# First FFT of a fused FFT-filter and squared-ReLU feed-forward kernel: later filter loads, crossed filter pieces by DMA, six zero matmuls, stage A of batch 1 in bank pairs

## The chip, the cores and the metric

The kernel runs on one core of a Trainium2 chip. Time is the device time of one launch in microseconds (us); the figure to be moved is the median over several launches. The core has five engines that run side by side, each through its own list of instructions in order: TensorE (PE, matmuls into PSUM), VectorE (DVE), ScalarE (ACT), GpSimd (POOL) and SyncE (SP). DMAs are issued from the lists of SP, ACT and POOL and carried by 16 DMA engines. A DMA issued by POOL can convert float32 to float16 on the way; one issued by SP can't. An instruction that waits for a semaphore holds back everything behind it in its engine's list.

## What is computed

The input `x` has 8 batches of 3008 tokens with 256 channels. Each batch is transformed along its tokens, multiplied by a complex filter, transformed back, and the result goes token by token through a feed-forward layer with a squared ReLU:

```python
def _attn_ref(x, filt_r, filt_i):
    X = np.fft.rfft(x, axis=1)
    F = (filt_r + 1j * filt_i)[None, :, :]
    Y = X * F
    y = np.fft.irfft(Y, n=x.shape[1], axis=1)
    return y.astype(np.float32)

def _moe_ref(x, w_in, w_out):
    h = np.maximum(x @ w_in, 0.0)
    return (h * h @ w_out).astype(np.float32)

# x (8, 3008, 256), filt_r and filt_i (1505, 256), w_in (256, 2048), w_out (2048, 256)
# out = _moe_ref(_attn_ref(x, filt_r, filt_i).reshape(24064, 256), w_in, w_out)
```

## The kernel before

**The transform.** 3008 = 64 x 47, so the transform is done in two steps, all by matmuls in float16. Stage A sums over the 47 (result `u`), stage B over the 64 (result in PSUM tile `psB`, with real and imaginary parts on the two halves of the partitions). `unit_b(b, p)` (L378) does stage B for two of the 24 frequency classes, p = 0 to 11, and multiplies by the filter tile `sF` into `prod`. `sF` is `[128, 2, 24, 256]`: in `sF[:, 0]` the real part lies on partitions 0 to 63 and the imaginary part on 64 to 127; in `sF[:, 1]` the two halves are crossed. Stage P (`unit_p0` for batch 0, `unit_p` for the others) goes back from frequencies, gives `ze`, and writes it to DRAM (`dZ`); `read_z` (L450) reads it back in another order into two tiles `zt`, and `unit_y` (L458) does the last step into `yt`, which holds a batch's transformed tokens.

**The feed-forward layer.** Tokens go in 47 groups of 512. Eight steps per group: `ffn_g1` (L486) makes 256 of the 2048 hidden channels in `psH`, ACT applies the ReLU (L506), DVE squares every second step (`ffn_sq`, L513); the output product of a group runs in the eight steps of the next group. Group 0's is `ffn_g2` (L515): step 8 uses the first half of `sWout`, step 9 the second half. Later groups use a seven-product scheme (`make_t`, `sums`, `products`). Group 0 needs units 0 to 3 of `unit_y`, the first step of group 1 needs units 4 to 7.

**The order of the work.** There is no scheduler: the order in which the code runs is the order of each engine's list. What is ahead of the loop at L741 is the prologue: batch 0's transform, three quarters of batch 1's stage A, and the first four `unit_y`. `fft_plan` (L641) puts all the other transform work at half steps of the loop: a unit with number r runs in step floor(r), in its first or second place. `fixed` units have their place; `moves` (loads, stores, small DVE work) ride along.

In detail, where the change touches it:

- **Loads at the start.** SP issues batch 0's input in six pieces of 512 KB (`load_wide`, L207; pieces go to the wide tiles `xw32[0]`, `[1]`, `[2]`, in the order of `HALVES`, L278), then the constants `sC1`, `sSB`, `sSP`, `sSPx` (L281 to L286). POOL's list begins with a one-element copy `tiny` (L288) that waits for the fourth of these pieces, the second half of `xw32[1]`, and holds POOL's list back until then. After it POOL issues the filter (`load_f`, L235: 18 DMAs, four class ranges `FC` = 0-6, 6-12, 12-18, 18-24), then batch 1's `x` (`load_x`) and the first half of `sWin`.
- **`turn_f`** (L245): two DVE copies of 64 partitions x 1536 elements fill `sF[:, 1]` for a range of classes from `sF[:, 0]`; called for a range just ahead of the first unit that uses it (p = 0, 3, 6, 9; L717 to L719).
- **`unit_b` for batch 0:** `psB` is copied to `ub` by ACT (L395), then DVE multiplies `ub` by both planes of `sF` (L397). `psB` takes its bank from `psF` where p % 4 is 0 or 1 and from `psO` where it is 2 or 3, two buffers each. `turn_u(k)` (L355) turns stage A's result for two p at a time and sits between the units on PE; `turn_u(2)` takes the two `psF` banks that units 0 and 1 had.
- **`settle_f`** (L251): once batch 0 has used `sF`, two DVE instructions per three classes rewrite it to the form the other batches use. All eight are `moves` in steps 1 to 8.
- **Stage A of batch 1:** `unit_a` (L316) does one of 16 slices: one matmul of 512 columns into one `psF` bank, one copy out, by ACT and DVE in turn; after each fourth slice the chunk `u` is written to DRAM (`write_u`). Slices 0 to 11 run in the prologue, 12 to 15 in steps 8 and 9. `bank_pair` (L163) hands out pairs of banks, in turn from `psH`, `psH`, `psF`, `psO`; `pair_engine` names ACT and DVE alternately.
- **`load_rest`** (L294) is behind `read_z` on POOL: a one-element copy waits for the first half of the first `zt`, then POOL issues the second half of `sWin`, the rest of batch 1's `x`, and the two halves of `sWout`.
- **`fill(n)`** (L303): n matmuls on a tile of zeros, whose result nothing reads.

Of the kernel before, what the change touches and what calls it, by code (L numbers as in the profile page):

```python
# [9 lines left out]
F16 = mybir.dt.float16  # L10
# [94 lines left out]
def kernel(  # L105
# [9 lines left out]
    nc = tc.nc  # L115
    B, S, D = x.shape
# [128 lines left out]
    def turn_f(c0, c1):  # L245

        for i in (0, 64):
            nc.vector.tensor_copy(out=sF[i:i + 64, 1, c0:c1, :],
                                  in_=sF[64 - i:128 - i, 0, c0:c1, :])

    def settle_f(c0, c1):  # L251

# [32 lines left out]
        load_const(sSP[:, c, :], dPA, k)  # L285
        load_const(sSPx[k], dPB, k)  # L286
    tiny = const.tile([1, 2], F16, name="tiny")
    nc.gpsimd.tensor_copy(out=tiny[:, 0:1], in_=xw32[1][0:1, 4, 0:1])  # L288
    for c in FC:
        load_f(*c)  # L290
    for k in range(2):
# [24 lines left out]
    def unit_a(b, a):  # L316

        c, i = divmod(a, 4)
        if i == 0:
            us[(b, c)] = p_u.tile([96, 8, D], F16, tag="u", name=f"u_{b}_{c}")  # L320
        ps = psF(f"psA_{b}_{a}")
        m = slice(2 * i, 2 * i + 2)
        nc.tensor.matmul(ps[0:96, :], sSA, x16s[(b, c)][0:94, m, :], start=True, stop=True)  # L323
        o = us[(b, c)][:, 2 * i:2 * i + 2, :]
        pv = ps[0:96, :].rearrange("p (a d) -> p a d", d=D)
        if a % 2 == 0 or b > 2:
            nc.scalar.copy(out=o, in_=pv)  # L327
        else:
            nc.vector.tensor_copy(out=o, in_=pv)
        if i == 3:  # L330
            write_u(b, c)

    def chunk_a0(k, *cs):

# [43 lines left out]
    def unit_b(b, p):  # L378
        if b == 0 and p % 4 > 1:
            ps = psO(f"psB_{b}_{p}").rearrange("p a d -> p (a d)")  # L380
        else:
            ps = psF(f"psB_{b}_{p}")
        for i in range(2):
            nc.tensor.matmul(ps[:, i * D:(i + 1) * D], sSB[:, 2 * p + i, :],  # L384
                             uts[b][:, 2 * p + i, :], start=True, stop=True)
        if b == 0:
            if p == 0:
                prods["ring"] = p_y.tile([128, 5, 2, 2, D], F16, tag="yt", name="prods_0")
            prod = prods["ring"][:, p % 5]
        else:  # L390
            prod = p_prod.tile([128, 2, 2, D], F16, tag="prod", name=f"prod_{b}_{p}")
        pv = ps.rearrange("p (a d) -> p a d", d=D)
        if b == 0:
            ub = p_prod.tile([128, 2, D], F16, tag="prod", name=f"ub_{p}")
            nc.scalar.copy(out=ub, in_=pv)  # L395
            pv = ub
        nc.vector.tensor_mul(  # L397
            out=prod,
            in0=pv.unsqueeze(1).to_broadcast([128, 2, 2, D]),
            in1=sF[:, :, 2 * p:2 * p + 2, :])  # L400
        prods[(b, p)] = prod
        if b > 0:
            for i in range(2):
                nc.gpsimd.dma_start(out=prod[64 * i:64 * i + 64, 0],  # L404
                                    in_=prod[64 - 64 * i:128 - 64 * i, 1],
                                    accum_op=mybir.AluOpType.add)
# [234 lines left out]
    def fft_plan():  # L641

        fixed, units, moves = [], [], []
        for b in range(1, B):
            f = (b * S // TG) * SLOTS - (48 if b > 1 else 40)
            d = 0
            if b == 1:
                for n in range(4, 16):
                    fixed.append(((n if n < 8 else n + 2 if n < 12 else 2 * n - 7) + n % 2 / 2,
                                  unit_y, 0, n))  # L650
                moves.append((7.5, read_z, 0, 3))
                for q in range(8):
                    moves.append((1 + q, settle_f, 3 * q, 3 * q + 3))
                moves.append((10, settle_sp))
                for a in range(12, 16):
                    fixed.append((2 + a / 2, unit_a, b, a))
                moves.append((10.5, read_u, b))
                d = 7
            else:
                for a in range(16):  # L660
                    if a % 2 == 0 and b > 2:
                        moves.append((f + ((-57 + 2.3 * a) if b == 3 else (-66 + 2.75 * a)),
                                      load_x, b, a // 2))
                    units.append((f + (-16 + a, -46 + 2.1 * a, -56 + 2.75 * a)[min(b, 4) - 2],
                                  unit_a, b, a))
                moves.append((f + (2 if b == 2 else -6.5), read_u, b))
            for p in range(12):
                r = 14 + 15 * p / 11 if b == 1 else 6 + 28 * p / 11 if b == 2 else -2 + 36 * p / 11
                units.append((f + r, unit_b, b, p))
                if b == 1 and 2 <= p < 10:  # L670
                    moves.append((f + r, load_x, 2, p - 2))
                units.append((f + r + (4.5 if b == 1 else 7 - 2.5 * p / 11), unit_p, b, p))
            for c in range(4):
                moves.append((f + (40 + d / 14, 43, 48, 54)[c] - d, read_z, b, c))
            for n in range(16):
                (fixed if n < 4 else units).append((f + YN[n] - d, unit_y, b, n))
        work, used, done = {}, set(), {}
        for r, *u in fixed:
            h = int(2 * r)
            used.add(h)  # L680
            work.setdefault(h, []).append(u)
        rank = (unit_b, unit_p, unit_y, unit_a)
        for r, *u in sorted(units, key=lambda u: (rank.index(u[1]), u[0])):
            after = done.get((u[0], u[1]), -1)
            h = min((h for h in range(max(int(2 * r) - 3, after + 1), int(2 * r) + 12)
                     if h not in used),
                    key=lambda h: (sum(h + i in used for i in (-2, -1, 1, 2)) > 2) * 2
                    + abs(h - int(2 * r)))
            used.add(h)
            done[(u[0], u[1])] = h  # L690
            work.setdefault(h, []).append(u)
        for r, *u in moves:
            work.setdefault(int(2 * r), []).append(u)
        return work
# [7 lines left out]
    for n, cs in enumerate(((0, 2), (0, 2), (1, 3), (1, 3))):  # L702
# [1 line left out]
            cast_wide(*h)  # L704
        chunk_a0(n % 2, *cs)
        if n < 2:
            fill(4 - 2 * n)
    uts[0] = p_ut.tile([128, NC, D], F16, tag="ut", name="ut_0")
    for k in range(2, 6):
        load_x(1, k)  # L710
    load_win(0)
    turn_u(0, nc.scalar, nc.vector)
    turn_u(1, nc.scalar, nc.vector)
    for k in range(8):
        if k < 6:
            for p in (2 * k, 2 * k + 1):
                for c in FC:  # L717
                    if c[0] == 2 * p:
                        turn_f(*c)  # L719
                if k > 1 and p % 2:  # L720
                    unit_p0(k - 2)
                unit_b(0, p)
# [4 lines left out]
    read_z(0, 0)  # L727
    read_z(0, 1)
    load_rest()
    for a in range(12):  # L730
        unit_a(1, a)
    fill(6)
    for n in range(4):
        unit_y(0, n)
    prologue[0] = False
# [53 lines left out]
```

## Time and profile before

| | us |
|---|---|
| median of 7 runs | 770.32 |
| lowest, highest | 769.25, 772.43 |
| the profiled execution, its own time | 771.0 |
| its span from first to last instruction | 769.2 |
| first feed-forward matmul (start of L502) | 52.18 |
| first matmul of group 0's output product (L522) | 65.98 |

| engine | busy us | share of the span |
|---|---|---|
| PE | 742.9 | 97% |
| DVE | 647.1 | 84% |
| ACT | 572.0 | 74% |
| POOL | 187.8 | 24% |

The mean granted clock of PE is 0.991 of full speed. The times above are counted from the start of the span, in the one profiled execution. All that the change edits lies in the first 78 us or so; from there on the span is the loop over groups. Between the span and the execution's own time lie 1.8 us.

### The profile page before, as it was taken

The page shows a single profiled execution, that of the slowest core. Times are in us where ns is not written, and L with a number is a line of the kernel's source. Part 1 is how long each engine was busy: PE and PEld are TensorE (multiplying, and loading weights), DVE is VectorE, ACT ScalarE, POOL GpSimd, SP SyncE. Part 2 cuts the span into 40 slices and gives each one's busy share as a digit, 9 for nine tenths or more (in the row PEclk, how much of TensorE's full clock was granted, in tenths as well). Part 3 has the DMA queues.
Part 4 walks back from the last instruction along what each step waited for, and adds up shares of the span by engine and source line. Part 5 has one row for each costly group of instructions (what it writes and reads, how often), then busy time and mean ns, then how long its engine had stood idle before and what let it go on. Part 6 is the DMA issues. An engine that isn't in the chain of part 4 may idle for free.

```text
span 769.2 us, 19455 instructions
## 1 busy us (share of the span) xinstructions
PE 742.9 (97%) x8138; PEld 544.3 (71%) x8138; DVE 647.1 (84%) x735; ACT 572.0 (74%) x842; POOL 187.8 (24%) x262
## 2 busy tenths in 40 slices
PE   6778999999999999999999999999999999999998
PEld 4535667777777777877778777787777777777776
DVE  4847998899889888898979889788989989888783
ACT  2756777788878887788877877778877777777773
POOL 3420561133303232223212324043311222000000
PEclk9989999999999999999999999999999999999999
DMA  9996798667676456855586565865447334321011
GB/s 314 174 213 142 163 182 211 203 115 142 134 203 143 100 120 148 214 118 94 125 214 136 104 135 103 200 144 118 101 105 209 91 77 97 96 71 55 29 57 56
DMA packets 107184, 104.87 MB, mean 136 GB/s; under 512 B 9960, under 2 KB 94504, under 8 KB 106200
## 3 DMA queue, kind: packets, MB, share of 16 engines
q1 hardware_dynamic: 82408, 77.80, 34.0%
q0 software_dynamic: 24544, 25.64, 24.4%
q8 instruction: 64, 1.05, 0.6%
q10 hardware_dynamic: 144, 0.18, 0.1%
q14 instruction: 24, 0.20, 0.1%
HBM read 58.95 MB, written 48.23 MB: 139 GB/s over the span
## 4 chain that ended last, share of the span: by engine, by line
PE 82%; DVE 9%; DMA 5%; ACT 2%; issue 1%; SPq 0%; POOL 0%; ACTq 0%; DVEq 0%
PE psH L502 36%; PE psX L615 18%; PE psY L615 14%; PE psA L323 3%; DMA zt<-dZ 3%; PE psY L472 2%; PE psB L384 2%; DVE h L513 2%; PE psP L436 2%; DVE prod L397 2%; PE psO L522 2%; PE fill L307 1%; DMA prod<-prod 1%; DVE sum L588 1%; ACT h L506 1%
## 5 line engine op out<-in xcount | busy, mean ns | idle before, releaser
L506 ACT ACTIVATE h<-psH 128x1024 f16<-128x1024 f32 x376 | 384.5, 1024 | 153.9 <-PE psH L502 151.8
L502 PE MATMUL psH<-yt,sWin 128*128 128x512 f16 (+7 forms) x1728 | 387.5, 352 | 3.6 <-DVE yt L481 2.9
L513 DVE TENSOR_TENSOR h<-h 128x2048 f16<-128x2048 f16 (+1 forms) x192 | 229.8, 1197 | 45.9 <-ACT h L506 45.6
L404 POOL DMA_DIRECT2D prod<-prod x168 | 139.4, 972 | 433.3 <-DVE prod L397 393.1
L502 PEld LDWEIGHTS <-sWin 128*128 128x128 f16 x1728 | 152.2, 98 | 100.3 <-issue 6.2
L615 PEld LDWEIGHTS <-sum 128*128 128x128 f16 x2880 | 177.6, 98 | 20.2 <-issue 0.3
L615 PEld LDWEIGHTS <-h 128*128 128x128 f16 x2160 | 133.7, 98 | 21.3
L397 DVE TENSOR_TENSOR prod<-psB,sF 128x1024 f16<-128x1024 f32 x84 | 102.4, 1219 | 14.5 <-PE psB L384 14.3
L615 PE MATMUL psX<-sT,sum 128*128 128x128 f16 x1440 | 102.4, 219 | 0.0
L615 PE MATMUL psY<-sT,sum 128*128 128x128 f16 x720 | 69.6, 219 | 0.0
L327 ACT CAST u<-psA 96x512 f16<-96x512 f32 x96 | 55.7, 580 | 6.2 <-PE psA L323 5.8
L591 DVE TENSOR_TENSOR sum<-sum,h 128x2048 f16<-128x2048 f16 x45 | 55.0, 1222 | 1.0
L615 PE MATMUL psY<-sWout,h 128*128 128x128 f16 x720 | 55.0, 219 | 0.0
L615 PE MATMUL psY<-sWout,sum 128*128 128x128 f16 x720 | 54.7, 219 | 0.2 <-DVE bot L630 0.2
L615 PE MATMUL psX<-sT,h 128*128 128x128 f16 x720 | 54.9, 219 | 0.0
L597 DVE TENSOR_TENSOR sum<-h,sum 128x2048 f16<-128x2048 f16 x45 | 54.8, 1217 | 0.0
L594 DVE TENSOR_TENSOR sum<-h 128x2048 f16<-128x2048 f16 x45 | 54.8, 1217 | 0.0
L588 DVE TENSOR_TENSOR sum<-h 128x2048 f16<-128x2048 f16 x45 | 54.7, 1216 | 0.0
L481 DVE CAST yt<-psY 128x376 f16<-128x376 f32 x62 | 33.7, 544 | 21.6 <-PE psY L472 21.6
L438 ACT CAST ze<-psP 128x512 f16<-128x512 f32 x84 | 49.1, 585 | 1.0 <-PE psP L436 0.7
L615 PE MATMUL psX<-sWout,h 128*128 128x128 f16 x720 | 47.6, 219 | 0.0
L472 PEld LDWEIGHTS <-zt 112*128 112x128 f16 x512 | 34.2, 99 | 18.3 <-issue 3.4
(70 smaller groups left out, 600.9 us busy)
## 6 DMA issues: line engine op xcount, KB each, us to landing
zt<-dZ SPq DMA_DIRECT2D x64, 192.0 KB
dU<-u SPq DMA_DIRECT2D x28, 384.0 KB
prod<-prod POOLq DMA_DIRECT2D x168, 64.0 KB, 2.8
dZ<-ze SPq DMA_DIRECT2D x28, 384.0 KB
x<-in_x_dram POOLq DMA_DIRECT2D x48, 192.0 KB, 5.0
ut<-dU SPq DMA_DIRECT2D x7, 1024.0 KB
out_dram<-top SPq DMA_DIRECT2D x31, 128.0 KB
out_dram<-bot SPq DMA_DIRECT2D x31, 128.0 KB
```

The lines of the kernel that those rows point to most:

```text
L327: nc.scalar.copy(out=o, in_=pv)
L397: nc.vector.tensor_mul(out=prod, in0=pv.unsqueeze(1).to_broadcast([128, 2, 2, D]), in1=sF[:, :, 2 * p:2 * p + 2, :])
L404: nc.gpsimd.dma_start(out=prod[64 * i:64 * i + 64, 0], in_=prod[64 - 64 * i:128 - 64 * i, 1], accum_op=mybir.AluOpType.add)
L472: nc.tensor.matmul(ps[:, 94 * jj:94 * jj + 94], zt[:, 4 * (g % 2) + jj, dt * 128:(dt + 1) * 128], sSY, start=True, stop=True)
L502: nc.tensor.matmul(ps[:, i, o:o + n], sWin[:, dt, jt * 128:(jt + 1) * 128], yts[b][:, dt, r:r + n], start=(dt == 0), stop=(dt == 1))
L506: nc.scalar.activation(out=h2[:, 2 * s:2 * s + 2, :], in_=ps, func=AF.Relu)
L513: nc.vector.tensor_mul(out=v, in0=v, in1=v)
L588: nc.vector.tensor_add(out=t, in0=a21, in1=a22)
L591: nc.vector.tensor_sub(out=t, in0=f[5], in1=a11)
L594: nc.vector.tensor_sub(out=t, in0=a11, in1=a21)
L597: nc.vector.tensor_sub(out=t, in0=a12, in1=f[6])
L615: nc.tensor.matmul(o[:, t, :], f[p][:, q, 128 * t:128 * t + 128], sg["w"][p][:, q, :], start=(m == 0 and p in (1, 2)), stop=(q == 7), skip ...
```

## The change

The edits, in the order of the program:

- `tiny` now waits for the sixth and last piece of batch 0's `x` instead of the fourth.
- `turn_f` for all four ranges is called once, ahead of the units of stage B. The first range is still copied by DVE; the other three become two DMAs each, issued from SP's list (six DMAs of 192 KB, SBUF to SBUF).
- `unit_b` for batch 0 runs one matmul on zeros (512 columns) into its bank ahead of the two real ones, for p = 0 to 5. For p = 0, 4 and 8 ACT's copy is left out and DVE multiplies straight from PSUM.
- Of the fills between the first chunks of stage A, four become three and two become one; the fill ahead of the first `unit_y` goes from six to four.
- Stage A's first twelve slices of batch 1 go through the new `chunk_a`: two slices share a pair of banks, and one engine empties a pair. The three `write_u` follow behind all of them.
- Five of the eight `settle_f` move into the prologue, behind `chunk_a` and ahead of the fill; the other three move from steps 6 to 8 to steps 9 to 11.

```diff
--- before.py
+++ after.py
@@ -245,8 +245,11 @@
     def turn_f(c0, c1):
 
         for i in (0, 64):
-            nc.vector.tensor_copy(out=sF[i:i + 64, 1, c0:c1, :],
-                                  in_=sF[64 - i:128 - i, 0, c0:c1, :])
+            o, v = sF[i:i + 64, 1, c0:c1, :], sF[64 - i:128 - i, 0, c0:c1, :]
+            if c0 == 0:
+                nc.vector.tensor_copy(out=o, in_=v)
+            else:
+                nc.sync.dma_start(out=o, in_=v)
 
     def settle_f(c0, c1):
 
@@ -285,7 +288,7 @@
         load_const(sSP[:, c, :], dPA, k)
         load_const(sSPx[k], dPB, k)
     tiny = const.tile([1, 2], F16, name="tiny")
-    nc.gpsimd.tensor_copy(out=tiny[:, 0:1], in_=xw32[1][0:1, 4, 0:1])
+    nc.gpsimd.tensor_copy(out=tiny[:, 0:1], in_=xw32[2][0:1, 4, 0:1])
     for c in FC:
         load_f(*c)
     for k in range(2):
@@ -329,6 +332,26 @@
             nc.vector.tensor_copy(out=o, in_=pv)
         if i == 3:
             write_u(b, c)
+
+    def chunk_a(b, c):
+
+        u = p_u.tile([96, 8, D], F16, tag="u", name=f"u_{b}_{c}")
+        us[(b, c)] = u
+        for k in range(2):
+            banks, groups = bank_pair(f"psA_{b}_{c}_{k}")
+            for i in range(2):
+                m = slice(4 * k + 2 * i, 4 * k + 2 * i + 2)
+                nc.tensor.matmul(banks[i][0:96], sSA, x16s[(b, c)][0:94, m, :],
+                                 start=True, stop=True)
+            eng = pair_engine()
+            for t, i in groups:
+                n = t.shape[1]
+                o = u[:, 4 * k + 2 * i:4 * k + 2 * i + 2 * n, :]
+                pv = t[0:96].rearrange("p t (a d) -> p (t a) d", d=D)
+                if eng is nc.scalar:
+                    eng.copy(out=o, in_=pv)
+                else:
+                    eng.tensor_copy(out=o, in_=pv)
 
     def chunk_a0(k, *cs):
 
@@ -380,6 +403,8 @@
             ps = psO(f"psB_{b}_{p}").rearrange("p a d -> p (a d)")
         else:
             ps = psF(f"psB_{b}_{p}")
+        if b == 0 and p < 6:
+            nc.tensor.matmul(ps, zero[:, 0:128], zero, start=True, stop=True)
         for i in range(2):
             nc.tensor.matmul(ps[:, i * D:(i + 1) * D], sSB[:, 2 * p + i, :],
                              uts[b][:, 2 * p + i, :], start=True, stop=True)
@@ -390,7 +415,7 @@
         else:
             prod = p_prod.tile([128, 2, 2, D], F16, tag="prod", name=f"prod_{b}_{p}")
         pv = ps.rearrange("p (a d) -> p a d", d=D)
-        if b == 0:
+        if b == 0 and p % 4:
             ub = p_prod.tile([128, 2, D], F16, tag="prod", name=f"ub_{p}")
             nc.scalar.copy(out=ub, in_=pv)
             pv = ub
@@ -649,8 +674,8 @@
                     fixed.append(((n if n < 8 else n + 2 if n < 12 else 2 * n - 7) + n % 2 / 2,
                                   unit_y, 0, n))
                 moves.append((7.5, read_z, 0, 3))
-                for q in range(8):
-                    moves.append((1 + q, settle_f, 3 * q, 3 * q + 3))
+                for q in range(5, 8):
+                    moves.append((4 + q, settle_f, 3 * q, 3 * q + 3))
                 moves.append((10, settle_sp))
                 for a in range(12, 16):
                     fixed.append((2 + a / 2, unit_a, b, a))
@@ -704,19 +729,18 @@
             cast_wide(*h)
         chunk_a0(n % 2, *cs)
         if n < 2:
-            fill(4 - 2 * n)
+            fill(3 - 2 * n)
     uts[0] = p_ut.tile([128, NC, D], F16, tag="ut", name="ut_0")
     for k in range(2, 6):
         load_x(1, k)
     load_win(0)
     turn_u(0, nc.scalar, nc.vector)
     turn_u(1, nc.scalar, nc.vector)
+    for c in FC:
+        turn_f(*c)
     for k in range(8):
         if k < 6:
             for p in (2 * k, 2 * k + 1):
-                for c in FC:
-                    if c[0] == 2 * p:
-                        turn_f(*c)
                 if k > 1 and p % 2:
                     unit_p0(k - 2)
                 unit_b(0, p)
@@ -727,9 +751,13 @@
     read_z(0, 0)
     read_z(0, 1)
     load_rest()
-    for a in range(12):
-        unit_a(1, a)
-    fill(6)
+    for c in range(3):
+        chunk_a(1, c)
+    for c in range(3):
+        write_u(1, c)
+    for q in range(5):
+        settle_f(3 * q, 3 * q + 3)
+    fill(4)
     for n in range(4):
         unit_y(0, n)
     prologue[0] = False
```

## The prediction

> **What bounds the kernel now.** I read the page's slices first, then busy time by stretch, then the first 80 us as timelines and as the chain of waits, then the DMA views.
>
> ```profile
> PE   6778999999999999999999999999999999999998
> DVE  4847998899889888898979889788989989888783
> PEclk9989999999999999999999999999999999999999
> DMA  9996798667676456855586565865447334321011
> ```
>
> Each digit is 19.2 us. PE has room in the first three or four slices only; behind them it is 90% busy, so a gain at the start should reach the end unless a later wait eats it. The DMA engines are full in the first three slices. In stretches (columns: length, busy us and count of PE, PEld, DVE, ACT, POOL, then granted clock, DMA share, GB/s):
>
> ```profile
> 48.00:52.00 4.00, 4.00 (x29) 2.77 (x28) 0.75 (x2) 0.82 (x2) 1.00 (x2) 0.50 1.07 195
> ...
> 60.00:65.00 5.00, 1.77 (x14) 0.74 (x12) 4.79 (x11) 2.42 (x4) 0.00 (x0) 1.00 1.24 250
> 65.00:70.00 5.00, 5.00 (x22) 2.76 (x21) 2.44 (x4) 1.84 (x3) 0.00 (x0) 0.66 0.10 23
> 70.00:75.00 5.00, 5.00 (x42) 3.48 (x40) 3.34 (x5) 3.79 (x6) 0.00 (x0) 1.00 0.46 122
> ```
>
> From 60 to 65 PE stands still and DVE is full; then PE works at a granted clock of 0.66. DVE's and PE's timelines show why:
>
> ```profile
> 61.59 1.22 DVE L513 TENSOR_TENSOR h<-h 128x2048 f16<-128x2048 f16 x1
> 62.82 0.36 DVE L253 TENSOR_SCALAR sF<-sF 64x768 f16<-64x768 f16 x1
> 63.21 0.35 DVE L255 COPY sF<-sF 64x768 f16<-64x768 f16 x1
> 63.58 0.36 DVE L253 TENSOR_SCALAR sF<-sF 64x768 f16<-64x768 f16 x1
> 63.97 0.35 DVE L255 COPY sF<-sF 64x768 f16<-64x768 f16 x1
> 64.36 0.55 DVE L481 CAST yt<-psY 128x376 f16<-128x376 f32 x1
> ```
> ```profile
> 64.96 0.81 PE L502 MATMUL psH<-yt,sWin 128*128 128x512 f16 x3 [2.68 <-DVE yt L481]
> ...
> 69.67 1.04 PE L522 MATMUL psO<-sWout,h 128*128 128x256 f16 x8
> ```
>
> PE waits 2.68 us for the copy of unit 7, which stands in DVE's list behind `settle_f`. The line at 69.67 is step 9, the first that needs the second half of `sWout`; I count the change up to it.
>
> **The change part by part.**
>
> *Later filter loads.* The fourth piece landed at 10.06 (start of `tiny`); two pieces of 0.52 MB at the 412 GB/s of the stretch 10 to 14 add 2.5 us, so POOL starts near 12.6, and all its loads stand behind that. In the old order no filter byte moved before 14 (SP's queue alone carried that stretch) and the two queues shared 14 to 20; a later start gives SP's constants those microseconds and the filter the following ones. The first range's last DMA was issued at 13.20 and took 8.6 us: there at 21.8, while DVE's copy of it starts at 24.16. Cost 0; bounds 0 and 2.5 less the cover of 2.3, so 0.2.
>
> *Crossed pieces by DMA.* Off DVE: six copies of 0.555 = 3.3 us. On SP: six issues of about 0.37 = 2.2 us, each waiting for its filter range; behind them wait the six `dZ` writes, the first of which was issued at 28.95, and then `read_z`. The last range's loads were issued by 25.4 and take some 4 us, so that write slips by 1 to 1.5 us at most, under the cover named below. The bytes: 6 x 0.197 = 1.18 MB, at 412 GB/s 2.9 us of all DMA engines. The stretch 20 to 28 carries 140 GB/s on average and its slices fall to one, two and four tenths at places, so I let about two thirds go in holes: loads behind are 0.9 us later. Bounds 0 and 2.9. The Trainium skill speaks against this edit (DMA: Bandwidth & Descriptors, "Issuing engines are not separate DMA queues"): DMAs of SP and POOL end up on the same 16 engines, so moving the issuer saves only sequencer time. By that rule without holes the loads slip by the whole upper bound.
>
> *Straight from PSUM.* Units 0, 4, 8: ACT loses 3 x 0.59, DVE pays 3 x (1.22 - 0.69) = 1.6, so DVE's net is 3.3 - 1.6 = 1.7 us less of a list that ran without a pause from 22.84 to 39.2. But the bank of unit 0 is now free only when DVE is through:
>
> ```profile
> 23.91 0.38 PE L361 MATMUL psT<-sC,uT 128*128 128x128 f16 x4
> ...
> 24.16 1.14 DVE L248 COPY sF<-sF 64x1536 f16<-64x1536 f16 x2
> ```
>
> The turn at 23.91 has to wait for the copy (to 25.3) and a product of 1.22: 26.5. Units 2 to 5 and the first `ze` stand behind it on PE. Following the lists with these durations, the first `ze` copy ends near 31.1 instead of 28.9, and from there ACT has 7.7 us of back-to-back copies and a 1.5 us tail with DVE: last `ze` at 40.3 instead of 41.2. Value -0.9; bounds +0.3 and -1.7.
>
> *Zero matmuls.* 6 x 0.22 = 1.3 us of PE, which is idle 5.5 of the 20 us from 20 to 40: cost 0, cover those gaps; up to 0.4 where they stand in the chain just told. A clock gain is not there to be had: the granted clock is 1.00 from 22.9 to 44. The fewer early fills (1 + 1 matmul) stand before waits for casts: 0.
>
> *Stage A in pairs, `settle_f` ahead.* After the last `ze` at 40.3 DVE has four copies at 0.69 and one pair at 1.22 (the nearest row for 1024 float32 columns), 4.0 us, then five `settle_f` at 0.75, 3.8 us: 48.1. The old serial ping-pong took until 48.2, then a fill held unit 0 to 50.04. Now unit 0 waits for `zt`. Its read was issued at 43.76, behind the last `dZ` write, and the bytes of both lie behind the loads of `x`; with 0.9 us of DMA delay against 0.9 us of earlier `ze` I take it unchanged, in time for a start at 47. DVE's list decides then: units 1 and 3 end at 49.6, where the old ones ended at 52.7. Feed-forward starts 3.2 us earlier; bounds 1 and 4.
>
> *Group 0.* Six `settle_f` stood ahead of unit 7's copy. Without them ACT's copies, 8 x about 1.03 plus two of 0.47, carry the group: first at 50.4, last to end at 59.2; group 1 can start at about 59.4 instead of 64.96: lead 5.5 us. The three left go beside `make_t`; DVE idles 2.6 of the 10 us in 70 to 80 and needs 2.2 more, of which it gives back the 0.7 of the one that ran at 66.07: hidden; if not, 1 us.
>
> *What is late next.* `sWout`:
>
> ```profile
> L273 POOL DMA_DIRECT2D sWout<-in_moe_w_out_dram x2: 916/920/925, 47.2 to 48.1; - x2
> ...
> DMA to landing us min/median/max: 13.6/16.0/18.4
> ```
>
> The halves landed at 60.8 and 66.5. Their issue hangs on the first half of `zt`, not on the feed-forward, and DMA is full from 47 to 65, so they don't come earlier by the lead: I take +0.3 for the second, 66.8 (0.9 of delay less 0.6 of earlier `ze`). Step 9, which could run at about 63.5, waits until then: 69.67 - 66.8 = 2.9 us of gain is left. PE's gap of 3 us is as long as the one in the old run, after which the clock stood at 0.66 for 5 us, or at half for 3.4. There that stretch ended before 69.67; now part of it falls behind step 9: between 0 and 1.7 us lost, I take 1.1.
>
> The Trainium skill (TensorE: Matmul & The Clock Gate, Part 1) wants an idle window of about 3.4 us before the clock is halved. This trace halved it after 2.68. By the page the gap might just pass unpunished, and the gain would be 2.9.
>
> **Sum** against the profiled execution, 771.0 with span 769.2: -2.9 + 1.1 = -1.8, so 769.2. The median shown is 0.7 below that execution; from 770.32 it is 768.5.
>
> **The rivals.**
>
> *Full lead.* The second half of `sWout` comes with the lead (less traffic ahead of it). For: `zt` might come earlier. Against: 4.04 MB at 213 GB/s between 47 and 66, all slices at nine. Step 9 at 64.5, no gap to halve the clock: -5.2, 765.1. Chance 0.10.
>
> *The change doesn't shorten the path.* The crossed pieces cost 1.5 to 2 us of DMA, the second half of `sWout` lands at 68.2, step 9 gains 1.5 and loses 1.1 to the clock: -0.4, 769.9. For: the DMA row. Against: the holes in 20 to 28. Chance 0.25.
>
> *Slower: DMA queues.* SP's packets take turns with POOL's:
>
> ```profile
> q0 software_dynamic: 360, 0.65, 88.6%
> q1 hardware_dynamic: 309, 0.16, 18.9%
> ```
>
> These are the counts of 33 to 37: nearly one for one, q1's half a kilobyte each. A crossed piece has rows of 1536 x 2 bytes, 3 KB, and one of these for each small filter packet would starve the filter and all of POOL's list behind it: `x`, `sWin`, then `dZ` and `zt`. From a delay of 2.0 us (69.67 - 66.5 - 1.1) the path is longer than before; I price it at 4 us (2.9 of bytes, the rest for a `dZ` write that lands late and holds `read_z`): +2.0, 772.3. For: every first slice of DMA is at nine. Against: the six are spread over 6 us. Chance 0.15.
>
> **How the numbers follow.** The forecast, 768.5, has 0.50; its own range, from a gain of 3.4 (no clock loss, `sWout` 0.5 early) to one of 0.5, is 766.9 to 769.8. 0.2% of 770, what a measurement of this kernel can tell from no change, is 1.5 us. The forecast's 0.50 splits into 0.36 faster, 0.11 within and 0.03 slower; the full lead is all faster; the second rival's 0.25 is 0.08, 0.15 and 0.02; of the slow case 0.13 is slower and 0.02 within. That makes 0.54 faster, 0.28 within, 0.18 slower. The range over the cases, with 2 in 10 left out: 765.2 to 772.0.
>
> **What would show it.** Right: the first L502 near 49.5; the gap before unit 7's copy gone; step 9's product waiting for `sWout`, first seen near 67; the last `ze` near 40; `sWout`'s second half landed near 66.8. Wrong: a product of unit 3, 6 or 9 waiting for a crossed piece (DVE idle on DMA between 27 and 37); `zt` later than 48; DVE late at 80, where its list is full (19.65 of 20 us from 80 to 100), so that the three moved `settle_f` show. If step 9 finds `sWout` there, the full lead is the case.

## The result, and the profile after

| | before | after |
|---|---|---|
| median, us (runs) | 769.89 (40) | 773.07 (17) |
| lowest, highest | 768.57, 772.43 | 770.47, 776.89 |
| first profiled execution, its span | 771.0, 769.2 | 770.91, 769.1 |
| last `ze` copy ends | 41.21 | 43.55 |
| first L502 (L527 after) | 52.18 | 51.46 |
| second half of `sWout` landed | 66.44 | 69.64 |
| step 9 | 69.67 | 69.69 |

The change is slower: ratio 1.0043, 95% interval 1.0032 to 1.0053, 3.2 us between the medians. The first profiled execution of the changed kernel lies at the low end of its runs, that of the kernel before at the upper side of its own (771.0, median 769.89). So the two show how the lead was lost, but not yet the 3.2 us; two more profiles below show more of it.

The slices of the changed kernel's page (19.2 us each): the third digit of PEclk is 7 instead of 8 and the fourth of DMA 8 instead of 6, the rest of these rows is nearly as before. On this scale the change can hardly be seen.

```profile
PE   6778999999999999999999999999999999999997
PEclk9979999999999999999999999999999999999999
DMA  9998798666676456855586565765447334321011
```

The stretches of the changed kernel (same columns as before):

```profile
48.00:52.00 4.00, 2.59 (x23) 2.05 (x24) 3.79 (x9) 0.94 (x2) 4.00 (x6) 0.58 0.98 225
60.00:65.00 5.00, 4.64 (x31) 2.25 (x28) 2.98 (x5) 4.48 (x7) 0.00 (x0) 1.00 1.32 237
65.00:70.00 5.00, 2.79 (x18) 1.69 (x17) 2.10 (x4) 2.95 (x4) 0.00 (x0) 1.00 0.69 140
70.00:75.00 5.00, 5.00 (x42) 3.47 (x40) 3.92 (x7) 2.64 (x4) 0.00 (x0) 1.00 0.47 114
```

PE works 4.64 us of the stretch 60 to 65 instead of 1.77: the gap before unit 7's copy is gone, as forecast. But the next stretch has 2.79 instead of 5.00. PE's timeline of the changed kernel says on what it stands:

```profile
66.03 1.03 PE L547 MATMUL psO<-sWout,h 128*128 128x256 f16 x8 [0.89 <-DMA sWout<-in_moe_w_out_dram]
...
69.69 1.03 PE L547 MATMUL psO<-sWout,h 128*128 128x256 f16 x8 [1.32 <-DMA sWout<-in_moe_w_out_dram]
```

Both halves of `sWout` are waited for. Their issues stand at 50.1 and 51.0, where they were at 47.2 and 48.1, because the gate of `load_rest` (second `tiny`) opened at 47.49 instead of 44.9. That goes back to `zt`, `dZ` and the last `ze`, and from there to DVE's timeline of the changed kernel:

```profile
29.28 0.69 DVE L422 TENSOR_TENSOR prods<-ub,sF 128x1024 f16<-128x1024 f16 x1 [0.86 <-DMA sF<-in_filt_i_dram]
...
32.22 0.68 DVE L392 CAST ut<-psT 128x512 f16<-128x512 f32 x1
35.22 1.29 DVE L422 TENSOR_TENSOR prods<-ub,sF 128x1024 f16<-128x1024 f16 x2 [2.31 <-DMA sF<-sF]
...
38.87 1.90 DVE L422 TENSOR_TENSOR prods<-ub,sF 128x1024 f16<-128x1024 f16 x3 [0.62 <-DMA sWin<-in_moe_w_in_dram]
```

Unit 3 waits 0.86, unit 6 waits 2.31 and unit 9 waits 0.62. The arrow names a crossed piece for unit 6 alone (classes 12 to 17). But by the semaphore events in the trace the second DMA of each crossed piece ends at 29.16, 35.10 and 38.74, and units 3, 6 and 9 start 0.12 to 0.13 later: all three wait for their pieces. In the kernel before there was no such pause: DVE made the piece of unit 6 itself in 1.14 us (32.30 to 33.44) and went on. So the chain is: crossed piece late, unit late, last `ze` late, `zt` late, gate late, `sWout` late, step 9 late. The experiments test its links.

### The profile page after: what moved, and what is told of

Same layout as the page of the kernel before. It is cut to its first block, busy times and chain, and to the rows that moved or that the text cites. A ratio compares the mean times of both kernels' runs of the same rounds, so it can differ in the third digit from the quotient of the medians.

```text
span 769.1 us, 19463 instructions
## 1 busy us (share of the span) xinstructions
PE 741.7 (96%) x8140; PEld 544.1 (71%) x8140; DVE 645.6 (84%) x728; ACT 570.0 (74%) x838; POOL 188.5 (25%) x262
## 4 chain that ended last, share of the span: by engine, by line
PE 80%; DVE 6%; DMA 6%; issue 1%; ACT 0%; SPq 0%; POOL 0%; DVEq 0%; ACTq 0%
PE psH L527 36%; PE psX L640 19%; PE psY L640 14%; DMA sWout<-in_moe_w_out_dram 2%; PE psY L497 2%; PE psA L326 2%; PE psB L409 2%; PE psP L461 2%; DVE prod L422 2%; DVE h L538 2%; PE psO L547 2%; DMA zt<-dZ 1%; DMA prod<-prod 1%; DVE sum L613 1%; DVE sum L619 1%
## 5 line engine op out<-in xcount | busy, mean ns | idle before, releaser
L527 PE MATMUL psH<-yt,sWin 128*128 128x512 f16 (+7 forms) x1728 | 388.6, 352 | 2.3 <-DMA sWin<-in_moe_w_in_dram 1.0
L527 PEld LDWEIGHTS <-sWin 128*128 128x128 f16 x1728 | 152.3, 98 | 100.0 <-issue 4.8
L640 PE MATMUL psY<-sT,sum 128*128 128x128 f16 x720 | 69.6, 219 | 0.0
L330 ACT CAST u<-psA 96x512 f16<-96x512 f32 x90 | 52.1, 579 | 2.7 <-PE psA L326 2.4
```

The lines of the kernel that those rows point to most:

```text
L527: nc.tensor.matmul(ps[:, i, o:o + n], sWin[:, dt, jt * 128:(jt + 1) * 128], yts[b][:, dt, r:r + n], start=(dt == 0), stop=(dt == 1))
L640: nc.tensor.matmul(o[:, t, :], f[p][:, q, 128 * t:128 * t + 128], sg["w"][p][:, q, :], start=(m == 0 and p in (1, 2)), stop=(q == 7), skip ...
```

## The experiments

All ratios are against the kernel before on the same chip, with 95% intervals. "Step 9" and other times in us are from the one profile of each kernel.

**One part undone.** First the crossed pieces, copied by DVE again ahead of their units:

```diff
-            if c0 == 0:
-                nc.vector.tensor_copy(out=o, in_=v)
-            else:
-                nc.sync.dma_start(out=o, in_=v)
+            nc.vector.tensor_copy(out=o, in_=v)
...
+                for c in FC:
+                    if c[0] == 2 * p:
+                        turn_f(*c)
```

> The changed kernel with one part undone: all four crossed filter pieces are DVE copies again, each ahead of its first unit. Theory (crossed pieces on the DMA engines delay the loads of x and sWin, then dZ and zt, then sWout): the second half of sWout lands 2 to 3 us sooner than 69.6, near 67, no unit waits for a crossed piece, the last ze ends near 41, time 769 to 770, some 3 to 4 us below the changed kernel, and the runs spread less. Rival (the later gate of the filter loads is the cost): less than 1 us below the changed kernel, 772 to 773.

770.91, ratio 1.0004 (0.9988 to 1.0020): the loss is gone. The last `ze` (42.86) and the second half of `sWout` (68.43) are still later than expected, though no unit waits for a crossed piece; the product straight from PSUM, below, costs that much at the last `ze`. Then the gate of the filter back on the fourth piece of `x`, crossed DMAs kept:

```diff
-    nc.gpsimd.tensor_copy(out=tiny[:, 0:1], in_=xw32[2][0:1, 4, 0:1])
+    nc.gpsimd.tensor_copy(out=tiny[:, 0:1], in_=xw32[1][0:1, 4, 0:1])
```

> The changed kernel with one part undone: the one-element copy ahead of the filter loads waits for the fourth piece of x again, so POOL's list starts 2.1 us sooner. Theory (crossed pieces): sWout lands at most 0.5 us sooner, time 772 to 773. Rival (gate): sWout lands 2 us sooner, time near 770.

771.83, ratio 1.0018 (1.0001 to 1.0035): part of it is back, between the two expectations (the second half of `sWout` landed at 68.58, 1.1 sooner). Both undone:

> The changed kernel with the crossed pieces copied by DVE again ahead of their units and the filter's gate back on the fourth piece of x; zero matmuls, units 0, 4, 8 straight from PSUM, pairs and settle_f stay. Theory (the crossed DMAs and the later gate carry all of the loss, each alone undone gave 1.0004 and 1.0018): ratio 0.999, near 769.7, step 9 at 67 to 67.6. Rival (the product straight from PSUM or the zero matmuls also cost, since unit 0's bank comes free later): ratio 1.002 or more, last ze at 42.5 or later.

769.93, ratio 1.0004 (0.9992 to 1.0017), no better than the crossed pieces undone alone; last `ze` at 42.59.

**One part alone, in the kernel before.** The same edits the other way round. Crossed pieces by DMA:

> The kernel before with one part of the change alone: three of four crossed pieces as DMAs on SP's list, all called ahead of the units. Theory (crossed pieces): zt and with it the issue of sWout 2 to 3 us later, second half of sWout at 68.5 to 70; but this kernel reaches step 9 only at 69.7, so +1 to +3 us, 771 to 773. Rival (gate): no difference, 769.5 to 770.5.

772.88, ratio 1.0036 (1.0018 to 1.0055): most of the loss, from this edit alone. The late gate:

> The kernel before with POOL's first instruction waiting for the sixth piece of x instead of the fourth, nothing else. Theory (a late filter costs nothing in the kernel before, its first class range landed at 20.97 in the changed kernel and 21.83 here, but x, sWin and zt behind it slip by 1 to 2 us against 3.2 us of slack at step 9): 770.4, ratio 1.0005. Rival (the gate costs what it seemed to in the changed kernel, where undoing it won 0.0025): ratio 1.002 or more.

769.48, ratio 1.0001 (0.9989 to 1.0012): nothing. Pairs, five `settle_f` and the shorter fill:

> The kernel before with stage A of batch 1 in bank pairs, five settle_f in the prologue and the fill of four; no other edit. If the gain side of the prediction was right (PE's 2.68 us gap goes, sWout then decides at 66.5 to 67): first L502 near 50.5, step 9 near 66.8, gain of 1.5 to 2.9, 767 to 768.4. If sWout does not come sooner than step 9 was in the kernel before: no gain, 769.5 to 770.5.

770.62, ratio 1.0001 (0.9987 to 1.0015). The lead is there, and it is not kept. PE's timeline of this kernel:

```profile
64.44 0.38 PE L323 MATMUL psA<-x,sC 94*96 94x512 f16 x1
67.53 1.03 PE L542 MATMUL psO<-sWout,h 128*128 128x256 f16 x8 [2.70 <-DMA sWout<-in_moe_w_out_dram]
...
129.16 0.33 PE L492 MATMUL psY<-sC,zt 112*128 112x94 f16 x4 [1.36 <-DMA zt<-dZ]
```

Step 9 could have run at 64.83 and waits for `sWout`; of the 2.2 us that are still won there (67.53 against 69.67; 82.30 against 84.51 at the first `psX`, the PSUM tile of group 1's output product), 1.5 go at 129, where the first `unit_y` of batch 1 waits for its own `zt`. Zero matmuls and the product straight from PSUM:

```diff
+        if b == 0 and p < 6:
+            nc.tensor.matmul(ps, zero[:, 0:128], zero, start=True, stop=True)
...
-        if b == 0:
+        if b == 0 and p % 4:
             ub = p_prod.tile([128, 2, D], F16, tag="prod", name=f"ub_{p}")
```

> The kernel before with the six zero matmuls and with units 0, 4 and 8 multiplied straight from PSUM, nothing else. Theory (unit 0's bank comes free later and the products cost DVE 3 x 0.53 on a full list): last ze at 42 to 42.6 instead of 41.2, all under the slack at step 9: ratio 1.000, 770.2. Rival (what the prediction said: the first ze later, the last one 0.9 earlier): last ze at 40.3, 769.9.

771.16, ratio 1.0017 (1.0005 to 1.0030), though its one profile (769.86) ended below the kernel before's: last `ze` at 41.21 and step 9 at 69.37. The start of stage B (first copy to `ut`) explains this. The kernel before:

```profile
22.22 1.07 ACT L367 CAST ut<-psT 128x512 f16<-128x512 f32 x2 [1.38 <-PE psT L361]
...
40.52 0.69 DVE L424 CAST ze<-psP 128x512 f16<-128x512 f32 x1 [1.30 <-ACT ze L423]
```

and this kernel:

```profile
20.63 1.07 ACT L367 CAST ut<-psT 128x512 f16<-128x512 f32 x2 [1.10 <-PE psT L361]
...
40.52 0.69 DVE L426 CAST ze<-psP 128x512 f16<-128x512 f32 x1 [1.30 <-ACT ze L425]
```

In this execution the clock was not halved near 18 (1.00 in the stretch 18.20 to 21.00, 0.50 in the kernel before's), so stage B began 1.59 earlier, and its last `ze` came at the same time. From the first `ut` to the end of the last `ze` it takes 20.58 instead of 18.99: 1.6 us more, near the 1.3 us of the ratio. So the theory had the delay about right, and its cover, the slack at step 9, was wrong. Which of the two edits costs this was not separated. Counted in the same way, the crossed pieces by DMA alone take 21.7, 2.7 us more, for a ratio worth 2.8 us.

**Bytes, or the wait for them?** The forecast had priced the crossed pieces by their bytes. So the kernel before got six more DMAs of the same bytes at the same place, with nobody waiting for the data:

```diff
+    def extra_f(c0, c1):
+        for i in (0, 64):
+            if c0 < 18:
+                o, v = sWout[i:i + 64, c0 - 6:c1 - 6, :], sF[64 - i:128 - i, 0, c0:c1, :]
+            else:
+                o = sWin[i:i + 64, :, 1024:1792]
+                v = sF[64 - i:128 - i, 0, c0:c1, :].rearrange("p (a b) d -> p a (b d)", a=2)
+            nc.sync.dma_start(out=o, in_=v)
...
+    for c in FC[1:]:
+        extra_f(*c)
     for k in range(8):
```

> The kernel before with the six crossed copies by DVE kept, and six more DMAs of the same bytes at the place where the change issues its own, from sF into parts of sWout and sWin that are loaded later: what they write is never read. Theory (the traffic and SP's held list cost, not the units' wait for the pieces): 772.5, ratio 1.003 to 1.004 as with the crossed pieces by DMA alone (1.0036); first dZ write near 31, last ze near 42. Rival (the units' wait for their pieces costs): 770.4, ratio 1.000, because no unit waits for these DMAs.

770.51, ratio 1.0001 (0.9990 to 1.0012), last `ze` at 41.22. My theory of that moment, traffic and a held list on SP, fell: in this kernel the bytes cost nothing. They did delay the loads: the last `dZ` write landed at 46.80 instead of 43.62, the gate of `load_rest` opened at 47.36 instead of 44.90, and the second half of `sWout` landed at 70.11 instead of 66.44. But step 9, at 70.16, waited only 0.26 for it: the kernel before has just the slack. The changed kernel has none, and there these DMAs that nobody waits for were not tried. DVE's waits of this kernel between 22 and 44 (line, releaser, us in total, times, longest) hold no DMA:

```profile
DVE ze L433 <- ACT ze L432: 1.3, 1, 1.3
DVE ut L378 <- ACT ut L376: 1.3, 1, 1.3
DVE u L338 <- PE psA L332: 1.1, 2, 0.7
```

**Where the 3.2 us go: two more profiles of the changed kernel.**

> The changed kernel once more, unaltered, for a second profile: its first one (770.91) lies at the low end of its own 17 runs (770.47 to 776.89). Theory (a unit that waits for its crossed piece sets the spread): units 3, 6 or 9 wait longer than in the first profile (0.86, 2.31, 0.62), last ze later than 43.55, and step 9 later than 69.69 by what the time is above 770.9. Rival (the spread arises behind step 9, at the reads of zt of later batches): step 9 within 0.5 of 69.7, and waits for zt near 130 and 500.

> As the run before it, a third profile of the changed kernel. Theory: time above 770.9 goes with a later last ze and a later step 9. Rival: with a wait for zt near 130 or 500, step 9 unmoved.

They ran 771.93 and 772.95. From the third profile, DVE's and PE's timelines:

```profile
32.72 0.68 DVE L392 CAST ut<-psT 128x512 f16<-128x512 f32 x1
36.65 1.29 DVE L422 TENSOR_TENSOR prods<-ub,sF 128x1024 f16<-128x1024 f16 x2 [3.25 <-DMA sF<-sF]
```
```profile
67.93 0.38 PE L326 MATMUL psA<-x,sC 94*96 94x512 f16 x1
71.06 1.87 PE L547 MATMUL psO<-sWout,h 128*128 128x256 f16 x8 [2.74 <-DMA sWout<-in_moe_w_out_dram]
72.72 0.63 PE L326 MATMUL psA<-x,sC 94*96 94x512 f16 x1
```

and its stretch from 70:

```profile
70.00:75.00 5.00, 3.94 (x22) 2.48 (x22) 1.61 (x2) 0.46 (x1) 0.00 (x0) 0.66 0.03 8
```

Here step 9 waits 2.74, and behind the wait the granted clock is halved: the eight products take 1.87 instead of 1.03, the stretch has a clock of 0.66. In the second profile it is the same with a wait of 3.95 (step 9 at 70.00). The first `psX` comes at 84.57, 86.15 and 87.13 in the three profiles (84.51 before), and their own times rise with it: 770.91, 771.93, 772.95. The rival, losses at later batches, is out for these three: none has a wait for `zt` near 130 or 500. Of the 17 runs, 12 lie above 772.95 and have no profile. The theory has one miss: in the second profile the last `ze` was earlier (41.95) than in the first. There the last `dZ` write took 4.1 us to land (2.4 in the first profile and in the kernel before), and the second half of `sWout` 19.8 (18.7 in the first profile). So not all of the delay comes from waiting units; slower DMAs are part of it, and how the loss divides between the two isn't shown.

**The need for the second half moved, no DMA touched.** Group 0's output product used the first half for block 0, the second half for block 0, and so on; now blocks 0 and 1 use the first half in steps 8 and 9, the second half in steps 10 and 11:

```diff
         t, half = divmod(s, 2)
+        swap = g == 0 and s < 4
+        if swap:
+            half, t = divmod(s, 2)
...
-                             sWout[:, jt, :], start=(jt == 0), stop=(jt == NJT - 1))
+                             sWout[:, jt, :], start=(jt == 0 and not (swap and t)),
+                             stop=(jt == NJT - 1), skip_group_check=swap)
```

In the changed kernel, in the kernel before, and in the kernel before with pairs and `settle_f`:

> The changed kernel with group 0's output product in the order that needs the second half of sWout in step 10 instead of step 9. Theory (all of the change's loss passes through that half, which landed at 69.64, 69.96 and 71.02 in three profiles of the changed kernel, with waits of 1.3 to 3.9 at step 9 and the half clock behind it): step 9 has no wait, step 10 one of 0 to 2, first psX at 82 to 84.5 instead of 84.6 to 87.1; 770 us, ratio 0.999 to 1.001. Rival (part of the loss lies elsewhere, at batch 1's zt or in group 1's start): ratio 1.002 or more.

> The kernel before with that order of group 0's output product alone. Theory (in the kernel before sWout is there when step 9 comes: 66.44 for 69.67): ratio 1.000, 770.1. Rival (the kernel before too waits for sWout in many of its runs, and the gain of 3 us of pairs, settle_f and this order together comes from this order alone): 0.997 or less.

> The kernel before with pairs and settle_f ahead, and group 0's output product in another order: steps 8 and 9 use the first half of sWout for both token blocks, steps 10 and 11 the second half. No DMA moves. Theory (the landing of sWout's second half, at 67.5, is what keeps the lead of 2 to 3 us): step 9 runs at 64.9 instead of 67.53, step 10's wait is under 1, the first psX at 80 to 80.8 instead of 82.3, 768.8. Rival (the lead is lost behind, at batch 1's zt near 129): first psX as the theory says, but the wait for zt at 129 grows by the same, and 770.3.

Changed kernel with it: 769.50, ratio 1.0000 (0.9983 to 1.0017). Kernel before with it: 770.08, 1.0002 (0.9993 to 1.0011). Pairs and `settle_f` with it: 767.34, 0.9961 (0.9939 to 0.9983). The edit is worth 0.0043 and 0.0040 where PE is early enough to wait, and nothing where it isn't. PE's timeline of the changed kernel with it:

```profile
65.68 1.04 PE L550 MATMUL psO<-sWout,h 128*128 128x256 f16 x8
...
70.05 0.33 PE L497 MATMUL psY<-sC,zt 112*128 112x94 f16 x4 [2.24 <-DMA zt<-dZ]
70.37 1.03 PE L550 MATMUL psO<-sWout,h 128*128 128x256 f16 x8
```

Step 9 runs at 65.68 with no wait; the next thing late is the third read of `zt`, which lands beside `sWout`.

**Is it the wait of the units, then?** If the crossed pieces cost the kernel before through `sWout` as well, the new order must take that back:

> The kernel before with the crossed pieces by DMA (1.0036 alone) and group 0's output product in the order that needs the second half of sWout two steps later. Theory (the crossed pieces cost through that landing, as in the changed kernel): ratio 1.000 to 1.0010, 770.3. Rival (in the kernel before, step 9 did not wait with them either, 70.29 for 70.33; the loss is a later feed-forward start by 0.6 to 1 and a late zt of batch 1, 1.38 at 132): ratio 1.002 to 1.004, first psX at 85 or later, a wait for zt at 130 to 132 as often as not.

772.87, ratio 1.0039 (1.0024 to 1.0053): the rival. DVE's timeline of this kernel, and of the kernel before at the same unit:

```profile
30.56 0.68 DVE L372 CAST ut<-psT 128x512 f16<-128x512 f32 x1
36.49 1.29 DVE L400 TENSOR_TENSOR prods<-ub,sF 128x1024 f16<-128x1024 f16 x2 [5.25 <-ACT ub L398]
```
```profile
32.30 1.14 DVE L248 COPY sF<-sF 64x1536 f16<-64x1536 f16 x2
33.55 1.29 DVE L397 TENSOR_TENSOR prods<-ub,sF 128x1024 f16<-128x1024 f16 x2
```

The trace names ACT's copy as releaser, but unit 6's `ub` was ready at about 29.1 and unit 7's at 31.0, so it is the other thing unit 6 needs, the crossed piece of classes 12 to 17. Its filter range had landed at 26.85, and its two DMAs were issued at 26.90 and 27.46; by the semaphore events in the trace they ended at 34.35 and 36.37, and unit 6 starts at 36.49. That is up to 8.9 us for one DMA, for a piece that DVE makes in 1.14. This profile (773.94) is the slowest of its six runs. From there everything is moved one for one: last `ze` 44.56 for 41.21, first `psY` 53.39 for 50.04, first L502 55.52 for 52.18, step 9 72.88 for 69.67. In the kernel before the serial stage A and unit 7's copy stand behind the last `ze`, so the delay needs no `sWout` to reach the end.

**Attempts to keep the lead.** The gate of `load_rest` on the last `ze` copy instead of on `zt`, in the kernel with pairs and `settle_f`:

```diff
-        nc.gpsimd.tensor_copy(out=tiny[:, 1:2], in_=ztiles[0][0:1, 0, 0:1])
+        nc.gpsimd.tensor_copy(out=tiny[:, 1:2], in_=zes[0][0:1, 23, 0:1])
```

> The kernel before with the pairs and the five settle_f ahead, and load_rest's gate on the last ze instead of the first half of zt (some 3 us earlier). Theory (the second half of sWout sets step 9, which waited 2.70 for it at 67.53): it lands near 64.5, step 9 at 65 to 65.5, 768.5. Rival (the earlier loads hold zt back, which the first unit_y waited 1.93 for at 47.5): first feed-forward matmul at 50.5 or later instead of 48.96, step 9 at 67 or later, 770.6.

769.12, ratio 0.9994 (0.9977 to 1.0011): no gain that can be told. `sWout`'s second half landed at 63.2, but `zt` now lies behind these loads. PE's timeline:

```profile
45.02 0.28 PE L490 MATMUL psY<-zero 128*128 128x128 f16 x2
52.68 0.47 PE L492 MATMUL psY<-sC,zt 112*128 112x94 f16 x4 [7.39 <-DMA zt<-dZ]
```

With batch 1's units drawn together on top, to bring its `zt` earlier:

```diff
-                r = 14 + 15 * p / 11 if b == 1 else 6 + 28 * p / 11 if b == 2 else -2 + 36 * p / 11
+                r = 14 + 14 * p / 11 if b == 1 else 6 + 28 * p / 11 if b == 2 else -2 + 36 * p / 11
...
-                moves.append((f + (40 + d / 14, 43, 48, 54)[c] - d, read_z, b, c))
+                moves.append((f + (40 + d / 14 - (b == 1), 43, 48, 54)[c] - d, read_z, b, c))
```

> As the kernel before with pairs, settle_f ahead and load_rest's gate on the last ze, and besides batch 1's units of stages B and P drawn together (14 steps for 15) with the first read_z one step earlier. Theory (the lead is given back at 129, where unit_y of batch 1 waited 1.36 for zt): no wait there, 767.2, 1.3 less than without. Rival (the give-back moves to the next wait, or the denser units cost as much): 768.5, no less.

769.84, ratio 1.0006 (0.9989 to 1.0024): no gain. And the same units drawn together with the new order of the product:

> As the run before it, and batch 1's units of stages B and P drawn together (14 steps for 15), first read_z of batch 1 one step earlier. Theory of two waits in a row (sWout, then batch 1's zt): no wait over 0.5 at 125 to 132, 767.5, ratio 0.9965. Rival (something else takes the gain): within 0.7 of the run before it.

768.15, ratio 0.9973 (0.9954 to 0.9991), with a wait of 1.47 for `zt` at 129.36 as before: the last `dZ` write of batch 1 was still issued at 119.55 from SP's list, behind the output stores, so it was no earlier. What would bring that `zt` sooner stays open. The best kernel once more, unaltered:

> The kernel before with pairs, settle_f ahead and the new order of group 0's output product, unaltered from its first run (767.34, ratio 0.9961, interval 0.9939 to 0.9983). Theory (a gain of 2 to 3 us that lasts): ratio 0.995 to 0.998. Rival (batch 1's zt takes it back in most runs): 0.9985 or more.

766.52, ratio 0.9965 (0.9952 to 0.9978). It is faster than both kernels, 2.7 us under the kernel before (median 769.18 beside it). Its PE timeline:

```profile
61.62 1.03 PE L545 MATMUL psO<-sWout,h 128*128 128x256 f16 x8 [0.24 <-DMA sWout<-in_moe_w_out_dram]
...
63.79 1.04 PE L545 MATMUL psO<-sWout,h 128*128 128x256 f16 x8
...
67.64 0.33 PE L492 MATMUL psY<-sC,zt 112*128 112x94 f16 x4 [1.73 <-DMA zt<-dZ]
```

Step 9 runs at 63.79, 5.9 us before the kernel before; 1.73 go to `zt` there, and the first `psX` is 3.9 early (80.60).

## Why the prediction was wrong

Forecast: faster, 768.5, range 765.2 to 772.0. Measured: slower, 773.07, outside the range. The step that failed is **"Crossed pieces by DMA"**: it priced SP's issues and the bytes ("about two thirds go in holes", 0.9 us) and took the pieces themselves as there in time. In the kernel before, the bytes cost nothing by themselves (1.0001); the edit with the wait of units 3, 6 and 9 costs 1.0036 to 1.0039. A DMA of a piece takes up to 8.9 us from issue, where the trace of before already had first-range filter loads at 8.6 us, its DMA slices at nine and, by its semaphore events, SP's first `dZ` write landing 10.8 us after issue (28.95 to 39.71). The bytes were too small a term as well: alone they moved the second half of `sWout` by 3.7 us, against 0.9 forecast and an upper bound of 2.9. That bound divides by the 412 GB/s of the stretch 10 to 14; at the 213 GB/s that the prediction reads from 47 to 66, with all slices at nine, it would be 5.5 us (an estimate from these two rows). In the changed kernel, where `sWout` decides, how much of the 3.2 us is the units' wait and how much the bytes stays open. The text itself named the sign ("a product of unit 3, 6 or 9 waiting for a crossed piece") and gave it no price.

Step by step:

- *Later filter loads*, cost 0: right. POOL started at 12.05 (forecast near 12.6), the first range landed at 20.97 (21.83 before), alone 1.0001. Beside the crossed DMAs it isn't free: undone there, the ratio went from 1.0043 to 1.0018, though those intervals touch.
- *Straight from PSUM*, last `ze` at 40.3: wrong, 41.95 to 43.95 in three profiles. The first `ze` ended at 30.45 (forecast near 31.1), so the start was right; what was missing are the waits behind it. In the first profile 13.1 us lie between the first `ze` and the last, of which units 3, 6 and 9 wait 3.8; the 9.3 left are the forecast's 9.2. Alone, with the zero matmuls and with the crossed copies still on DVE, the edit costs 1.6 us at the last `ze`, and 1.0017.
- *Stage A in pairs, `settle_f` ahead*: right in kind. Feed-forward started 0.7 us earlier in the changed kernel, less than the forecast 3.2 because `zt` was late; with pairs and `settle_f` alone it started at 48.96, 3.2 earlier, and in the changed kernel with the crossed copies on DVE at 50.83.
- *Group 0*, unit 7's gap gone: right; group 1's matmuls that waited until 64.96 before came at 64.12 (forecast 59.4), for the same lateness of `zt`, and for the second half of `sWin`, waited for with 0.98 at 59.06. Three sums here and in the next step do not close: the ACT copies from 50.4 end at 59.6, not 59.2; step 9 could run at 63.5 in one place and at 64.5 among the rivals; and `sWout` is given 0.6 of earlier `ze` where 0.9 was worked out. None of them turns the forecast.
- *What is late next*: right place, wrong time. Step 9 waits for the second half of `sWout`, at 69.6 to 71.0 instead of 66.8. Without the crossed pieces (pairs alone) it landed at 67.48 and step 9 ran at 67.53.
- *Clock loss of 1.1 behind the gap*: in two of three profiles, at 1.2 to 1.3 (from step 9 to the first `psX` 16.1 us in both, 14.9 in the first profile). By the Trainium skill (TensorE: Matmul & The Clock Gate, Part 1) it takes a window of about 3.4 us; here it came after 2.74 and 3.95, and after 2.70 in the kernel with pairs it did not come; the last section shows where they differ.
- *The rival "Slower: DMA queues"*, 772.3 with a chance of 0.15, had the sign, and a size 1.2 us too small (2.0 of 3.2 between the medians). Its mechanism, packets that starve POOL's list, is half right: that list did slip (gate of `load_rest` at 47.4 with the extra DMAs, 44.9 without), but in the kernel before this was covered. The skill's rule weighed under the crossed pieces (DMA: Bandwidth & Descriptors, "Issuing engines are not separate DMA queues"), that DMAs of all issuers end on the same 16 engines, agrees with that run: six DMAs from SP's list delayed the loads that POOL issues.

The parts are not a sum. Pairs alone and the new order alone are worth nothing (1.0001, 1.0002), together 0.9961 and 0.9965: each removes one of two waits in a row. Between the two kernels with the new order (1.0000 against 0.9961) lie the crossed pieces, the gate, the zero matmuls and the product straight from PSUM together; alone in the kernel before the pieces cost 1.0036, the gate 1.0001, the last two 1.0017.

## What to carry to other kernels

A copy that moves from an engine to a DMA must be priced by its latency, from issue to landing at the load of that stretch, against the first instruction that needs it, before bytes or issue slots are counted. When an edit wins a lead, look for the next load that sets a step, and ask whether the order of use can be changed in place of the order of loads: here two steps of eight products exchanged were worth some 3 us, where opening the gate earlier only moved the wait from `sWout` to `zt`. A single profile at the low end of its runs shows the chain, not the size of a loss.

## What the runs showed of the hardware

- In the kernel before with crossed pieces by DMA and the new order, the 192 KB DMAs of the pieces landed 3.9 to 8.9 us after issue while POOL's queue was busy; in its stretch 27 to 36 the DMA engines stood at nine in nearly every slice, at 209 GB/s.
- Inside the span the halved clock lasts a multiple of 3.41 us in every profile here, but the gap that brings it isn't fixed: 2.68 (kernel before), 2.74 and 3.95 (changed kernel) and 2.32 (drawn-together units with the new order) did, 2.70 (pairs) and 2.24 (changed kernel with the new order) did not. A gap of 1.72 near 18 did in the kernel before and did not in the kernel before with the new order.
- What decides can be told from the 20 profiles. Within each, all changes of the clock lie multiples of 3.41 us apart, so they cut the span into equal stretches. At full clock, every stretch in which PE was idle for more than 1.75 us was followed by the halved clock, and none with less than 1.60 idle (counted from 8 us on: 51 halvings, 4291 stretches without; between 1.60 and 1.75 both occur). The gap of 2.68 lies whole in one stretch; the gap of 2.70 is cut by a boundary at 66.06. The kernel before, then the pairs (columns as before):

```profile
62.24:65.65 3.41, 0.73 (x5) 0.36 (x4) 3.28 (x7) 0.18 (x1) 0.00 (x0) 1.00 1.06 208
```
```profile
62.65:66.06 3.41, 2.17 (x14) 1.25 (x13) 1.99 (x4) 2.73 (x4) 0.00 (x0) 1.00 1.12 210
66.06:69.47 3.41, 1.95 (x13) 1.27 (x13) 0.66 (x2) 0.07 (x1) 0.00 (x0) 1.00 0.03 8
```

- The changed kernel's runs spread over 6.4 us, the kernel before's over 3.9. In the three profiles of the changed kernel the difference is the landing of `sWout` against step 9. In other kernels batch 1's `zt` cost 0.75 to 1.64 us at 126 to 132 in some of the profiles and nothing in others: of two profiles of the best kernel, with leads of 5.0 and 3.9 us, the one lost 1.44 there and the other nothing.
